# Attention and a gated FFN on one core: fill and first eight slots put in one written step order

## Chip, cores and metric

The kernel runs on one core of a Trainium2 chip. The metric is device time in microseconds for one execution, the median of five runs. The core's engines are named as in the profile: PE is the matrix engine, PEld its weight load, DVE the vector engine, ACT the scalar engine, POOL the GpSimd engine and SP the sync engine. Here POOL mostly issues the input loads, and SP mostly issues transposing transfers and the output.

## What is computed

Two stages follow each other. The first is an attention of two parts on q, k and v of 8 batches, 8 heads, 576 positions and width 64: a full attention on positions averaged by fours, whose output is repeated four times, and a local one in which a position sees those less than four away. Their sum is x, with 4608 rows of 512. The second stage is an FFN with a gate.

```python
def _attn_ref(q, k, v):
    q_d = q.reshape(B, H, Sd, factor, D).mean(axis=3)
    ...
    out_up = np.repeat(sm_attn(q_d, k_d, v_d), factor, axis=2)
    mask = np.abs(pos[:, None] - pos[None, :]) < factor
    scores = np.where(mask, scale * np.matmul(q, k.transpose(0, 1, 3, 2)), -1000000000.0)
    ...
    return (out_up + np.matmul(attn, v)).astype(np.float32)

def _moe_ref(x, w_gate, w_val, w_out):
    gate = np.maximum(x @ w_gate, 0.0)
    val = x @ w_val
    return (gate * val @ w_out).astype(np.float32)
```

`factor` is 4, `d_model` 512 and `d_ff` 1536.

## The kernel before

Two heads make a pair, so there are 32 pairs; four pairs give all 512 columns of x for one batch, 576 tokens. The FFN works on 9 chunks of 512 tokens. A pair goes through these steps:

- **Loads**, on POOL's queue: q and k (for pairs 0 to 8 one transfer each, from pair 9 on one for each head), v in overlapping blocks (`vw`), and from pair 9 on a second copy of v (`v4`) that POOL sums by fours (`emit_v2`, `emit_v1`). Below pair 9 PE does the pooling of v instead, with six matmuls (`emit_vd`, L373) and an ACT copy (L380). The constants `NTP = 9` and `NVP = 9` set the two borders. The weights come in slices, w_gate and w_val in four each (`emit_wslice`, each slice for three of the 12 row blocks jj of the FFN), w_out in four (`emit_wo`).
- **Transposes** of q and k: for pairs 0 to 8 on PE (`emit_qkT_pe`, L328: 24 matmuls into three PSUM banks, with the pooled columns beside the wide ones), evicted by ACT and DVE in six copies (L348 the pooled, L350 the wide ones); from pair 9 on by a transposing transfer from SP (L302), and DVE pools (L309).
- **Scores** (`emit_s1_mm`, L389 and L400), exponentials on ACT (L410 twice for the local part, L424 once for the pooled one, `ed`), the band masks on DVE (L416 twice).
- **Sums**, in one of three forms. For pairs 0 to 3, the fill, `emit_s2`: matmuls with the exponentials as the stationary side (L447 and L456), DVE's reciprocals and products (L464, L465, L472, L474), then `emit_x_pe` transposes x on PE (L601, L605) and copies it to `xT` (L614, L615, L617). For pairs 4 to 8 `emit_s2t`: denominators and numerators side by side (L486 to L514), ln and exp on ACT for the inverse (L523, L525), a product on DVE (L528). From pair 9 on `emit_s2w_mm`, one matmul group for both (L552, L560) with ln, exp and product on L570, L575 and L579. `emit_xsum` (L538) adds the repeated part into `xT`.

A block jj of the FFN is four matmuls with w_gate (hg) and four with w_val (hv), all L622, a relu on ACT (L639) and a gate product on DVE (L643) into `gT`. The output y is 12 matmuls for 128 tokens (L652) in chunk 0; from chunk 1 on it is made by units of seven smaller products with prepared sums (L712, L718), for which DVE prepares differences of w_out halves once (`emit_wt`, L685).

The order of the work is written by functions in the first part. `emit_fill` runs pairs 0 to 3 one after the other, each with loads for four pairs ahead, scores, sums, the next pair's transposes, and matmuls on zeros (`emit_warm`, L825, 512 columns into bank 7) as fillers. `emit_slot` runs slots 0 to 7, one a pair, with three jj blocks of chunk 0 in slots 0 to 3 and of chunk 1 in slots 4 to 7, and the outputs of chunk 0 in slots 4 to 7; slot 7 ends with the list `LEAD_IN`. From slot 8 on the list `ORDER` gives the step order of all engines for two slots at a time (`emit_periods`), and `TAIL` that of the end. Each engine runs its own instructions in the order in which they are written. Queues of loads are POOL's own order.

Outputs of chunk 0 are issued from ACT (`nc.scalar` in `emit_y`); those of units from SP. PSUM has eight banks; the fill uses bank 2 to 5 for scores, 2 to 4 for the transposes of the next pair, 6 for v and the pooled sums, and 0 and 1 for the local sums and for x.

Of the kernel before, what the change touches and what calls it, by code (L numbers as in the profile page):

```python
# [17 lines left out]
LEAD_IN = """  # L18
hg/3 relu/3 o/b00 o/b01 o/b10 o/b11 ln/b0 ln/b1 hv/3 gate/3 inv/b hg/4 relu/4 hv/4 xn/b0 gate/4
hg/5 relu/5 hv/5 xn/b1 xsum/b  # L20
# [35 lines left out]
LATE = ("gate/5/1", "next/0/1", "next/1/1")  # L56
# [61 lines left out]
def kernel(  # L118
# [26 lines left out]
    NVP = 9  # L145
# [10 lines left out]
    ffn = ctx.enter_context(tc.tile_pool(name="ffn", bufs=3))  # L156
# [38 lines left out]
    q32 = q32full[0:96]  # L195
    gT = ring(2, [128, NJJ, TCH], FP16, "gT_")
# [3 lines left out]
    wt4 = [xT[:, 0:3, 0:TCH].rearrange("p k (h d) -> p k h d", h=2)]  # L200
    wt4 += [t.rearrange("p (k h) d -> p k h d", h=2) for t in wtnew]
# [42 lines left out]
    def emit_load_qk(hp):  # L244
        for i in range(4):
            emit_load_q1(hp, i)

    def emit_load_q1(hp, i):

        b, off = head_off(hp)  # L250
        src, dst, hh = (q, k)[i // 2], qk16[hp % NL][:, i // 2, :], i % 2
        if hp < NTP:
            if hh:
                return
            if hp == 0 and src is q:
                nc.sync.dma_start(
                    q32.rearrange("p (n d) -> p n d", d=64),
                    _dap(src, off, [[D, 96], [NQ * D, 2 * NB], [1, D]]),
                )
                nc.scalar.copy(out=dst, in_=q32)  # L260
            else:
                nc.gpsimd.dma_start(
                    dst.rearrange("p (n d) -> p n d", d=64),
                    _dap(src, off, [[D, 96], [NQ * D, 2 * NB], [1, D]]),
                )
            return
        nc.gpsimd.dma_start(  # L267
            dst.rearrange("p (j h d) -> p j h d", h=2, d=64)[:, :, hh, :],
            _dap(src, off + hh * S * D, [[D, 96], [NQ * D, NB], [1, D]]),
        )  # L270
# [45 lines left out]
    def emit_qkT_pe(hp, b0, b1, b0_last=False):  # L316
        r, r4, r2 = hp % NL, hp % 4, hp % 2
        sv = qk16[r].rearrange("p i (h j d) -> p i h j d", h=2, d=64)
        blocks = list(range(2 * NB))
        if hp == 0:  # L320
            blocks = blocks[NB:] + blocks[:NB]
        elif b0_last:
            blocks = blocks[4:] + blocks[:4]
        for n in blocks:
            lo = 120 * (n % 4)
            bank = b0 if n < 4 else b1 + n // 4 - 1
# [8 lines left out]
        big = qkT[r4][:, 0 : 2 * S].rearrange("p (b n t) -> p b n t", b=3, n=4)  # L335
        sml = qkd[r2].rearrange("p i t -> p (i t)").rearrange("p (b n t) -> p b n t", b=3, n=4)
        act, dve = nc.scalar.copy, nc.vector.tensor_copy
        if hp == 0:
            plan = ((2, 1, act), (2, 0, act), (1, 1, dve), (1, 0, dve), (0, 1, act), (0, 0, dve))
        elif b0_last:  # L340
            plan = ((1, 1, act), (1, 0, act), (2, 1, dve), (2, 0, dve), (0, 1, dve), (0, 0, act))
        else:
            plan = ((0, 1, act), (0, 0, act), (1, 1, dve), (2, 1, dve), (2, 0, dve), (1, 0, act))
        for i, pooled, copy in plan:
            bank = b0 if i == 0 else b1 + i - 1
            t = ps[:, bank, 0:480].rearrange("p (n t) -> p n t", n=4)
            if pooled:
                copy(out=sml[:, i], in_=t[:, :, 96:120])  # L348
            else:
                copy(out=big[:, i], in_=t[:, :, 0:96])  # L350
# [16 lines left out]

    def emit_vd(hp, bank):
        t = vw[hp % NL][:, :, 0:64].rearrange("p (h j) d -> p j h d", h=2)
        o = ps[:, bank, 0:256].rearrange("p (c h d) -> p c h d", c=2, h=2)  # L370
        for c in range(2):
            for sig in range(3):
                nc.tensor.matmul(  # L373
                    out=o[:, c, :, :],
                    lhsT=pool_sb[0:WK, sig, :],
                    rhs=t[:, 3 * c + sig, :, :],
                    start=(sig == 0),
                    stop=(sig == 2),
                )
        nc.scalar.copy(  # L380
            out=vd[hp % 3].rearrange("p c (x d) -> p c x d", x=3)[:, :, 0:3:2, :], in_=o[0:72]
# [49 lines left out]
    def emit_s1(hp, p0):  # L431
        emit_s1_mm(hp, p0)
        for g in range(2):
            emit_exp(hp, p0, g)
            emit_mask(hp, g)
        emit_ed(hp, p0)

    def emit_s2(hp, bank, pu):
        r2 = hp % 2
        x = xo[hp % 3]  # L440
        vflat = vw[hp % NL].rearrange("p b c -> p (b c)")
        for hh in range(2):
            for tcx in range(2):
                for c in range(2):
# [4 lines left out]
                        lhsT=ed[r2][:, hh, s0 : s0 + 128],  # L449
# [3 lines left out]
                    )  # L453
        for hh in range(2):
            for j in range(NB):
                nc.tensor.matmul(  # L456
                    out=ps[:, 2 * pu + hh, 65 * j : 65 * j + 65],
                    lhsT=ee[r2][:, hh, NQ * j : NQ * j + 128],
# [4 lines left out]
        rd = small.tile([72, 2, 2], FP32, name="rd", tag="rd")  # L463
        nc.vector.reciprocal(out=rd, in_=_sap(ps, (0, 72), 512 * bank + 64, [[66, 2], [65, 2]]))  # L464
        nc.vector.tensor_tensor(  # L465
            out=x[0:72, NB : NB + 2, :].rearrange("p t (h d) -> p h t d", h=2),
            in0=_sap(ps, (0, 72), 512 * bank, [[131, 2], [65, 2], [1, 64]]),
            in1=_sap(rd, (0, 72), 0, [[2, 2], [1, 2], [0, 64]]),
            op=ALU.mult,
        )  # L470
        ru = small.tile([96, 2, NB], FP32, name="ru", tag="ru")
        nc.vector.reciprocal(out=ru, in_=_sap(ps, (0, 96), 1024 * pu + 64, [[448, 2], [65, NB]]))  # L472
        for j0, j1 in ((0, 3), (3, 6)) if hp == LEAD - 1 else ((0, 6),):
            nc.vector.tensor_tensor(  # L474
                out=x[:, j0:j1, :].rearrange("p j (h d) -> p h j d", h=2),
                in0=_sap(ps, (0, 96), 1024 * pu + 65 * j0, [[513, 2], [65, j1 - j0], [1, 64]]),
                in1=_sap(ru, (0, 96), j0, [[NB, 2], [1, j1 - j0], [0, 64]]),
                op=ALU.mult,
            )

    def emit_s2t_mm(hp, den, num):
        r2 = hp % 2
        e, d = ee[r2], ed[r2]
        for g in range(2):
            for hh in range(2):
                nc.tensor.matmul(  # L486
                    out=ps[64 * hh : 64 * hh + 64, den + g, 0:288],
                    lhsT=ones_sb[0:WK, 0:64],
                    rhs=e[:, hh, 288 * g : 288 * g + 288],
# [3 lines left out]
            for c in range(2):  # L493
                for hh in range(2):
                    nc.tensor.matmul(
                        out=ps[64 * hh : 64 * hh + 64, den + g, 288:360],
                        lhsT=ones_sb[0:72, 64:128],
                        rhs=d[:, hh, c * SD + 72 * g : c * SD + 72 * g + 72],
                        start=(c == 0),
                        stop=(c == 1),  # L500
                    )
        for g in range(2):
            for j in range(3):
                for hh in range(2):
                    nc.tensor.matmul(
                        out=ps[64 * hh : 64 * hh + 64, num + g, NQ * j : NQ * j + NQ],
                        lhsT=vw[hp % NL][:, NB * hh + 3 * g + j, 0:64],
                        rhs=e[:, hh, 288 * g + NQ * j : 288 * g + NQ * j + NQ],
                        start=True,
                        stop=True,  # L510
                    )
            for c in range(2):
                for hh in range(2):
                    nc.tensor.matmul(  # L514
                        out=ps[64 * hh : 64 * hh + 64, num + g, 288:360],
                        lhsT=vd[hp % 3][:, c, 128 * hh : 128 * hh + 64],
                        rhs=d[:, hh, c * SD + 72 * g : c * SD + 72 * g + 72],
                        start=(c == 0),
                        stop=(c == 1),
                    )  # L520

    def emit_rden(den, between=lambda: None):
        nc.scalar.activation(out=rden, in_=ps[:, den : den + 2, 0:360], func=AF.Ln)  # L523
        between()
        nc.scalar.activation(out=rden, in_=rden, func=AF.Exp, scale=-1.0)  # L525
# [3 lines left out]

    def emit_s2t(hp, between):  # L530
        emit_s2t_mm(hp, 4, 2)
        emit_rden(4, between)
        emit_xn(2)
        emit_xsum(hp)
# [51 lines left out]
    def emit_s2w(hp):  # L586
        for hh in range(2):
            for g in range(2):
                emit_s2w_mm(hp, hh, g)
        for hh in range(2):  # L590
            emit_ln(hh)
        emit_inv()
        for hh in range(2):
            emit_xnw(hh)

    def emit_x_pe(hp, pp):
        b, kk = hp // NPB, hp % NPB
        x = xo[hp % 3]
        for g in range(2):
            flat = pair(pp)[:, g, 0:288]  # L600
# [595 lines left out]
```

## Time and profile before

| | |
|---|---|
| median of 5 runs | 348.01 us (346.79 to 348.7) |
| profiled execution | 348.01 us, span 346.0 us |
| PE / DVE / ACT / POOL busy | 336.7 / 293.3 / 215.3 / 192.6 us |
| L622 with w_val / w_gate | 432 and 352 matmuls of 512 columns |
| chain that ended last | PE 84%, DVE 9%, ACT 3%, DMA 2% |
| granted PE clock | 1.000 |
| loads on the software queue (POOL) | 22.93 MB |

A row of a timeline is: start in us, length in us, engine, line, operation, output, inputs, count. A row can merge several instructions of one kind; its length then runs from the first start to the last end, and since an engine begins the next instruction before the last has wholly ended, differences of starts are the better price of an instruction on a full engine. A row of the chain of waits is start, length and the step that held the end at that time. A row of the issue table gives the transfers under way in the stretch asked for, and the time from issue to landing.

### The profile page before, as it was taken

What the parts mean: (1) busy time and instruction counts of PE and PEld (TensorE: products, weight loads), DVE (VectorE), ACT (ScalarE), POOL (GpSimd) and SP (SyncE); (2) the same over time, 40 slices, a digit from 0 to 9 for tenths busy, and PEclk for the clock granted to TensorE, in tenths of its full rate; (3) what the DMA queues carried; (4) which work ended last, traced back from release to release, by engine and by line L of the source; (5) the groups of instructions that cost most, each with busy time, mean ns of one, the idle gap of its engine ahead of it and who ended that gap; (6) DMA issues with size and microseconds to landing.
All of it is one profiled execution on the core that took longest, in us unless ns stands there. A gap on an engine that the chain in (4) does not pass through costs nothing.

```text
span 346.0 us, 8159 instructions
## 1 busy us (share of the span) xinstructions
PE 336.7 (97%) x3187; PEld 210.5 (61%) x3187; DVE 293.3 (85%) x529; ACT 215.3 (62%) x410; POOL 192.6 (56%) x233
## 2 busy tenths in 40 slices
PE   6899999999999999999999999999999999999996
PEld 2665555555565756565666556665766557767685
DVE  5895567788899999999999999999999798786892
ACT  3767776677667776577667766776677634344222
POOL 8986556899989997989298869840300000000000
PEclk9999999999999999999999999999999999999999
DMA  9999999999999999999989998992000001011023
GB/s 151 166 171 186 186 190 160 170 149 189 185 142 188 116 171 120 135 150 145 120 108 164 132 133 77 176 114 66 31 32 31 32 0 47 30 33 52 32 69 109
DMA packets 168774, 40.31 MB, mean 117 GB/s; under 512 B 150080, under 2 KB 165664, under 8 KB 168736
## 3 DMA queue, kind: packets, MB, share of 16 engines
q0 software_dynamic: 132960, 22.93, 92.6%
q1 hardware_dynamic: 35056, 15.79, 23.8%
q10 hardware_dynamic: 720, 1.08, 1.0%
q8 instruction: 25, 0.41, 0.5%
q14 instruction: 13, 0.11, 0.1%
HBM read 46.45 MB, written 9.44 MB: 162 GB/s over the span
## 4 chain that ended last, share of the span: by engine, by line
PE 84%; DVE 9%; ACT 3%; DMA 2%; issue 1%; ACTq 0%; POOLq 0%
PE ps L622 45%; PE ps L718 18%; PE ps L928 4%; PE ps L652 3%; PE ps L552 3%; DVE xo L712 2%; PE ps L328 2%; PE ps L389 2%; PE ps L400 2%; DMA qk<-in_k_dram 2%; PE ps L560 1%; DVE gT L643 1%; ACT rden L570 1%; DVE xn L579 1%; DVE xo L474 1%
## 5 line engine op out<-in xcount | busy, mean ns | idle before, releaser
L622 PE MATMUL ps<-xT,wv_sb 128*128 128x512 f16 x432 | 109.3, 379 | 0.1
L622 PE MATMUL ps<-xT,wg_sb 128*128 128x512 f16 x352 | 89.1, 380 | 0.1
L639 ACT ACTIVATE r<-ps 128x512 f16<-128x512 f32 x88 | 52.3, 595 | 28.2 <-PE ps L622 28.0
L643 DVE TENSOR_TENSOR gT<-r,ps 128x512 f16<-128x512 f16 x88 | 59.2, 681 | 11.6 <-ACT r L639 6.3
L622 PEld LDWEIGHTS <-wv_sb 128*128 128x128 f16 x432 | 41.0, 98 | 41.9 <-issue 0.6
L622 PEld LDWEIGHTS <-wg_sb 128*128 128x128 f16 x352 | 32.0, 98 | 32.3 <-DVE xT L615 0.6
L579 DVE TENSOR_TENSOR xn<-ps,rden 64x720 f16<-64x720 f32 x46 | 41.7, 906 | 6.6 <-ACT rden L575 5.5
L410 ACT ACTIVATE ee<-ps 112x576 f16<-112x576 f32 x64 | 38.1, 648 | 10.4 <-PE ps L400 9.3
L570 ACT ACTIVATE rden<-ps 64x720 f32<-64x720 f32 x46 | 35.2, 765 | 14.9 <-PE ps L560 13.9
L267 POOL DMA_DIRECT2D qk<-in_q_dram x46 | 33.9, 742 | 5.0 <-DMA wo_sb<-in_moe_w_out_dram 2.9
L361 POOL TENSOR_TENSOR vd<-v 72x256 f16<-72x256 f32 x23 | 19.8, 872 | 28.7 <-PE ps L560 28.2
L267 POOL DMA_DIRECT2D qk<-in_k_dram x46 | 33.9, 741 | 2.6 <-DMA v<-in_v_dram 1.1
L416 DVE TENSOR_TENSOR ee<-ee,cst_sb 112x576 f16<-112x576 f16 x64 | 31.3, 511 | 3.0 <-ACT ee L410 2.2
L718 PEld LDWEIGHTS <-gT 128*128 128x128 f16 x288 | 28.2, 98 | 8.6
L292 POOL DMA_DIRECT2D vw<-in_v_dram x30 | 28.7, 956 | 8.4 <-PE ps L622 2.9
L355 POOL TENSOR_TENSOR v<-v 72x512 f32<-72x512 f16 x23 | 31.5, 1370 | 2.0 <-DMA v<-in_v_dram 1.5
L309 DVE TENSOR_REDUCE qkd<-qkT 128x288 f16<-128x1152 f16 x23 | 30.9, 1343 | 0.0
L718 PEld LDWEIGHTS <-xo 128*128 128x128 f16 x240 | 22.6, 98 | 8.1 <-issue 1.7
L752 ACT COPY q<-ps 128x256 f32<-128x256 f32 x39 | 14.5, 372 | 18.8 <-PE ps L718 18.5
L718 PE MATMUL ps<-wo_sb,gT 128*128 128x256 f16 x192 | 24.9, 273 | 0.0
L538 DVE TENSOR_TENSOR xT<-xn 128x576 f16<-128x576 f16 x28 | 24.1, 860 | 0.6
L938 ACT COPY vw<-ps 128x256 f32<-128x256 f32 x30 | 10.8, 374 | 20.7 <-PE ps L928 13.8
(115 smaller groups left out, 572.1 us busy)
## 6 DMA issues: line engine op xcount, KB each, us to landing
out_dram<-y_sb SPq DMA_DIRECT2D x20, 256.0 KB, 3.6
vw<-in_v_dram POOLq DMA_DIRECT2D x30, 168.0 KB, 6.9
qk<-in_q_dram POOLq DMA_DIRECT2D x46, 72.0 KB, 6.2
qk<-in_k_dram POOLq DMA_DIRECT2D x46, 72.0 KB, 6.4
v<-in_v_dram POOLq DMA_DIRECT2D x23, 144.0 KB, 6.6
out_dram<-y_sb SPq DMA_DIRECT2D x22, 128.0 KB, 1.7
wg_sb<-in_moe_w_gate_dram POOLq DMA_DIRECT2D x4, 384.0 KB, 9.6
wv_sb<-in_moe_w_val_dram POOLq DMA_DIRECT2D x4, 384.0 KB, 10.8
```

The costliest lines, as they stand in the source:

```text
L267: nc.gpsimd.dma_start(dst.rearrange("p (j h d) -> p j h d", h=2, d=64)[:, :, hh, :], _dap(src, off + hh * S * D, [[D, 96], [NQ * D, NB], [ ...
L292: nc.gpsimd.dma_start(t, _dap(v, base, [[D, WK], [NQ * D, n], [1, D]]))
L309: nc.vector.tensor_reduce(out=qkd[hp % 2].rearrange("p i t -> p (i t)"), in_=qkT[hp % 4][:, 0 : 2 * S].rearrange("p (t f) -> p t f", f=4), ...
L355: nc.gpsimd.tensor_tensor(out=m, in0=t[:, :, 0:128], in1=t[:, :, 128:256], op=ALU.add)
L410: nc.scalar.activation(out=o, in_=ps[0:WK, p0 + 2 * g : p0 + 2 * g + 2, 0:288], func=AF.Exp, scale=scale)
L416: nc.vector.tensor_tensor(out=o, in0=o, in1=_sap(masks_sb, (0, WK), 288 * g, [[0, 2], [1, 288]]), op=ALU.mult,)
L570: nc.scalar.activation(out=rden[lo : lo + 64], in_=ps[de : de + 64, 4 + 2 * hh : 6 + 2 * hh, 0:360], func=AF.Ln)
L579: nc.vector.tensor_tensor(out=xn[lo : lo + 64], in0=ps[lo : lo + 64, 4 + 2 * hh : 6 + 2 * hh, 0:360], in1=rden[lo : lo + 64], op=ALU.mult,)
L622: nc.tensor.matmul(out=pair(pp)[:, which, :] if out is None else out, lhsT=w[:, kk, bass.ts(jj, 128)], rhs=xT[:, kk, c * TCH : (c + 1) * TCH],
L639: nc.scalar.activation(out=r1, in_=pair(pp)[:, 0, :] if h1 is None else h1, func=AF.Relu)
L643: nc.vector.tensor_tensor(out=gT[c % 2][:, jj, :], in0=r1, in1=pair(pp)[:, 1, :] if h2 is None else h2, op=ALU.mult)
L718: nc.tensor.matmul(out=out, lhsT=left[:, i, :], rhs=right[i], start=(first and i == 0), stop=(i == NK - 1), skip_group_check=True,)
```

## The change

The two lists of functions (`emit_fill`, `emit_slot`, `emit_slot_in`, `LEAD_IN`) are replaced by one list, `FRONT`, in which every step of the fill and of slots 0 to 7 stands by itself: its kind, the pair or jj block, the part, and the PSUM bank. `emit_front` reads it in order. Steps that carry an @ are those of `ORDER`, with the half and the chunk. The list's beginning, which covers the fill and the start of chunk 0, and some later pieces:

```diff
+FRONT = """
+pads loadk/0 loadv/0 loadq/1 loadk/1 loadv/1 loadq/2 cast loadk/2 tr/0/2/4 tr/0/1/3 ev/0/21V/4
+loadv/2 tr/0/0/2 ev/0/20V/4 ev/0/11A/3 vd/0/6 ev/0/01A/2 ev/0/00A/2 loadq/3 vc/0/6 ev/0/10A/3
+warm/6 tr/1/0/7 loadk/3 ev/1/01A/7 ev/1/00A/7 warm/3 tr/1/1/0 loadv/3 s1/0/2 ev/1/11A/0
+ev/1/10A/0 tr/1/2/1 ed/0/2 wg/0 ev/1/20V/1 ex/0/0/2 warm/4 sd/0/6 ev/1/21V/1 wv/0 rd/0/6
+ex/0/1/2 warm/2 s1/1/0 td/0/6 ma/0/0 ones/4 vd/1/6 ex/1/1/0 ma/0/1 loadq/4 warm/2 su/0/4 ed/1/0
+ru/0/4 ex/1/0/0 tu/0/1/4 loadk/4 warm/3 tr/2/1/2 tr/2/2/3 tu/0/0/4 ev/2/10A/2 tr/2/0/0 loadv/4
+ev/2/20V/3 ev/2/11A/2 xp/0/1/5 ev/2/01A/0 xp/0/0/4 ev/2/00A/0 ev/2/21V/3 xe/0/1V/5 vc/1/6 ones/5
+warm/2 s1/2/0 ma/1/1 xe/0/0A/4 ma/1/0 sd/1/6 loadq/5 ex/2/1/0 su/1/4 rd/1/6 td/1/6 ed/2/0 ru/1/4
...
+ex/3/0/0 warm/2 hv/0/0/7 wv/1 hv/0/1/7 tu/2/0/4 ex/3/1/0 hv/1/0/1 hv/1/1/1 ma/3/0 xp/2/0/4
+ones/6 vc/3/6 ma/3/1 xp/2/1/5 xe/2/0A/4 sd/3/6 xe/2/1V/5 tr/4/0/0 loadq/6 rd/3/6 su/3/4
+ev/4/00A/0 td/3/6 tr/4/1/2 ru/3/4 ev/4/01A/0 loadk/6 hg/0/0/6 tu/3/0/4 ev/4/11A/2 hg/0/1/6
+ev/4/10A/2 hv/1/2/1 tu/3/1/4 hg/1/0/0 loadv/6 tr/4/2/3 xp/3/0/4 ev/4/21V/3 xp/3/1/5 xe/3/0A/4
+hg/0/2/6 wg/2 xe/3/1V/5 hg/1/1/0 hg/1/2/0 ev/4/20V/3 hg/0/3/6 wv/2 hg/1/3/0 relu/0/6 hv/0/2/7
+hv/0/3/7 s1/4/2 relu/1/0 gate/0/7 loadq/7 hv/1/3/1 ed/4/2 vd/4/6 hv/2/*/7 ex/4/0/2 ex/4/1/2
+hg/3/*/0 loadk/7 vc/4/6 ma/4/1 tr/5/1/3 ma/4/0 relu/3/0 tr/5/0/2 tr/5/2/4 ev/5/00A/2 hg/2/*/6
+ev/5/21V/4 gate/1/1 ev/5/01A/2 loadv/7 ev/5/10A/3 num/4/0/2 ev/5/20V/4 relu/2/6 vd/5/1 den/4/1/5
+wg/3 vc/5/1 gate/2/7 den/4/0/4 ev/5/11A/3 hv/3/*/1 ln/4 wv/3 num/4/1/3 inv gate/3/1 tr/6/1/0
+s1/5/4 loadq/8 xn/2 tr/6/2/1 ed/5/4 ev/6/21V/1 hg/4/*/2 ex/5/0/4 ev/6/20V/1 ex/5/1/4 loadk/8
...
```

A tr step is a third of a pair's transposes, ev an eviction (block, pooled or not, A for ACT or V for DVE, bank), s1 scores, ex, ed and ma the exponentials and masks, vd and vc the pooling of v and its copy, sd and su the two kinds of sums of the fill, rd, td, ru and tu its reciprocals and products, xp and xe the transposed x and its copy by halves, den and num the two halves of the second form of the sums.

Further on, the loads of w_out stand as wo/0, wo/1, wo/2, then q and k of pair 9, then wo/3, v of pair 8 and v of pair 9. The other edits:

```diff
-LATE = ("gate/5/1", "next/0/1", "next/1/1")
+LATE = ("gate/5/1", "gate/4/1", "next/0/1", "next/1/1")
...
-    NVP = 9
+    NVP = 11
...
-    wt4 = [xT[:, 0:3, 0:TCH].rearrange("p k (h d) -> p k h d", h=2)]
-    wt4 += [t.rearrange("p (k h) d -> p k h d", h=2) for t in wtnew]
+    wt4 = [t.rearrange("p (k h) d -> p k h d", h=2) for t in wtnew]
+    wt4 += [xT[:, 0:3, 0:TCH].rearrange("p k (h d) -> p k h d", h=2)]
...
+    def emit_flip(hp, i, bank):
+        sv = qk16[hp % NL].rearrange("p i (h j d) -> p i h j d", h=2, d=64)
+        for n in range(4 * i, 4 * i + 4):
...
+    def emit_flipped(hp, i, pooled, eng, bank):
...
+        t = ps[:, bank, 0:480].rearrange("p (n t) -> p n t", n=4)
+        copy_on(eng)(out=o[:, i], in_=t[:, :, 96:120] if pooled else t[:, :, 0:96])
...
+    def emit_tu(hp, g, bank):
+        j = 3 * g
+        nc.vector.tensor_tensor(
+            out=xo[hp % 3][:, j : j + 3, :].rearrange("p j (h d) -> p h j d", h=2),
...
+    def emit_x_out(hp, g, eng, bank):
+        lo = hp // NPB * S + 288 * g
+        copy_on(eng)(out=xT[:, hp % NPB, lo : lo + 288], in_=ps[:, bank, 0:288])
...
-        emit_out(c, ty, y_sb, nc.scalar)
+        emit_out(c, ty, y_sb, nc.sync)
...
-    def emit_warm(n):
+    def emit_warm(n, wide=False):
         for _ in range(n):
             nc.tensor.matmul(
-                out=ps[:, 7, :], lhsT=zero_sb[:, 0:128], rhs=zero_sb[:, 128:640], start=True, stop=True
-            )
+                out=ps[:, 7, :] if wide else ps[:, 6, 264:512],
+                lhsT=zero_sb[:, 0:128],
+                rhs=zero_sb[:, 128 : 640 if wide else 376],
...
+    def emit_front(tok):
+        kind, *a = tok.split("/")
+        if "@" in tok:
+            emit_step(kind, a[0], *map(int, a[1].split("@")))
         else:
...
+            FRONT_STEPS[kind](*[int(x) if x.isdigit() else x for x in a])
...
-        emit_warm(10)
-        emit_qkT_pe(0, 2, 3)
-        emit_pads()
-        emit_warm(3)
-        for hp in range(LEAD):
-            emit_fill(hp)
-        gate = None
-        for s in range(PS):
-            gate = emit_slot(s, gate)
+        emit_warm(12, True)
+        for tok in FRONT.split():
+            emit_front(tok)
         emit_periods(PS // 4, (NP - LEAD) // 4)
```

The list also holds the loads that `ORDER` had placed ahead of slot 8, so `emit_periods` starts at its own first chunk. `ORDER` and `TAIL` keep their text; the second gate product of a chunk, gate/4, now comes from `ORDER` at the chunk's border too, as gate/5 did before. The buffers of the relu and of the reciprocals become fixed rings of three and two.

## Prediction before the result was known

> **What bounds the kernel now.** I read the page's head and shares first, then a table of busy time by stretches.
>
> ```profile
> span 346.0 us, 8159 instructions
> PE 336.7 (97%) x3187; PEld 210.5 (61%) x3187; DVE 293.3 (85%) x529; ACT 215.3 (62%) x410; POOL 192.6 (56%) x233
> ...
> 14.40:18.40 4.00, 3.79 (x78) 2.86 (x78) 3.91 (x11) 3.10 (x8) 4.00 (x5) 1.00 1.63 191
> 18.40:22.40 4.00, 3.80 (x78) 2.87 (x78) 3.91 (x11) 3.05 (x8) 3.19 (x5) 1.00 2.13 167
> 46.00:54.60 8.60, 8.60 (x106) 4.56 (x103) 5.76 (x13) 6.82 (x14) 4.52 (x6) 1.00 1.38 200
> 87.00:95.50 8.50, 8.50 (x70) 4.35 (x65) 7.29 (x10) 6.32 (x10) 8.48 (x12) 1.00 1.70 184
> ```
>
> The columns after the length are PE, PEld, DVE, ACT, POOL busy, clock, DMA. From 27 us on PE is bound by its own work (8.60 of 8.60). In the fill, rows one and two, PE looks busy, but part of it are matmuls on zeros; there DVE is full: 3.91 of 4.00. So the front can gain only in the fill, and loses wherever the new order makes PE wait later. DVE's timeline over one pair of the fill:
>
> ```profile
> 16.58 0.17 DVE L464 RECIPROCAL rd<-ps 72x4 f32<-72x4 f32 x1
> 16.78 0.42 DVE L465 TENSOR_TENSOR xo<-ps,rd 72x256 f16<-72x256 f32 x1
> 17.12 0.22 DVE L472 RECIPROCAL ru<-ps 96x12 f32<-96x12 f32 x1
> 17.38 0.95 DVE L474 TENSOR_TENSOR xo<-ps,ru 96x768 f16<-96x768 f32 x1
> 18.25 0.81 DVE L416 TENSOR_TENSOR ee<-ee,cst_sb 112x576 f16<-112x576 f16 x2
> 19.09 0.76 DVE L617 CAST xT<-ps 128x576 f16<-128x576 f32 x1
> 19.76 0.41 DVE L348 CAST qkd<-ps 128x96 f16<-128x96 f32 x2
> 20.09 0.55 DVE L350 CAST qkT<-ps 128x384 f16<-128x384 f32 x1
> 20.55 0.17 DVE L464 RECIPROCAL rd<-ps 72x4 f32<-72x4 f32 x1
> ```
>
> Each starts as the one before ends; the pace is 20.55 - 16.58 = 3.97 us a pair. Start differences are the prices below: pair of masks 0.84, numerators 0.87, xT 0.67, two pooled evictions 0.33, a wide one 0.46. The ends of the two halves of the front, from the chain of waits and PE's timeline:
>
> ```profile
> 26.89 0.47 DVE xT L615
> 27.40 0.61 PE ps L622 x2
> ...
> 95.53 0.82 PE L718 MATMUL ps<-wo_sb,gT 128*128 128x256 f16 x6
> ```
>
> Pair 3's x is complete at 27.36; the first matmul behind slot 7 starts at 95.53. All behind that keeps its text, so the forecast is where this start moves to. The profiled execution took 348.01 us, which is also the median of the runs; 2.0 us of it lie around the span. Loads, from POOL's timeline and the issue table of two short windows:
>
> ```profile
> 4.14 0.88 POOL L262 DMA_DIRECT2D qk<-in_k_dram  x1
> qk<-in_k_dram POOLq DMA_DIRECT2D x1, 144.0 KB, 5.6
> ...
> 19.40 0.83 POOL L794 DMA_DIRECT2D wg_sb<-in_moe_w_gate_dram  x1
> wg_sb<-in_moe_w_gate_dram POOLq DMA_DIRECT2D x1, 384.0 KB, 9.4
> ```
>
> Pair 1's k lands at 4.14 + 5.6 = 9.74, the second w_gate slice at 19.40 + 9.4 = 28.8. POOL's order is unchanged as far as pair 8's k, so these times hold for the changed kernel.
>
> **The first pair of the fill.** In the new order PE takes two of pair 1's transposes ahead of pair 0's scores, and the second reads k. So the scores wait: 9.74 + 0.25 (8 of 24 transposes at 0.75) = 10.0, against 8.89. Then ACT, from its starts: pair 1's two evictions 0.57 after transposes and latency, to 10.8; exp of ed 0.55; two exps 0.55 and 0.65, to 12.55; last mask 13.25; 12 matmuls 0.38 and latency, 13.85; reciprocal 0.25; two half numerators 0.47 each (the two at 24.83 took 0.94). That is 15.05, against 14.35 (13.40 + 0.95): **0.7 lost**, and queued behind it is all of DVE's work for pair 1.
>
> **The pace.** Of a pair's 3.97 DVE gives one pooled eviction to ACT (-0.16) and half of xT (0.67 to 0.39, -0.28); splitting the numerators costs 0.94 for 0.87 (+0.07): 3.60. Pairs 1 and 2 take 7.20, pair 3, with no wide eviction before its numerators, 2.97: 25.2. Its x blocks share banks with the numerators, so both run after: two of 0.25, latency 0.15, xT 0.46: 26.3. **Gained 1.05** on 27.36. ACT, at 3.1 of 4.0, takes what DVE gives (0.14 + 0.40) and is at 3.6, as full as DVE: that cover is thin (first rival).
>
> **Work taken forward.** By 27.40 PE had done 6 matmuls of the first FFN chunk (3 w_val, 3 w_gate); the new order has 11 before pair 3's x: 5 x 0.216 = **1.08 gained**. It is possible because the partial sums get banks 7, 1, 6, 0.
>
> **Work added.** Pairs 9 and 10 pool v on PE: 2 x 0.34 (6 matmuls, from the chain) = 0.68 lost, and two ACT copies of 0.37 beside it. Pair 8 takes the form with 20 matmuls in 0.79 instead of 0.89: -0.10. POOL loses two v4 loads and two pairs of sums (2 x (0.74 + 1.17 + 0.88) = 5.6 us) and the DMA queue 288 KB; PE waited for none of these, so nothing. Each switch from 128-wide work to 64-wide (scores, transposes, pooled sums) costs PE 0.09 (36.26 after 1.83 for 1.74 of matmuls); I count 17 before behind 27.4 and 21 after: +0.36.
>
> **Waits added.** Behind pair 3 the order is followed with the same prices. hg/3 stands before hg/2 and needs the slice that lands at 28.8; PE reaches it at 26.3 + 9 x 0.216 + scores 0.5 + v pooling 0.34 + a switch 0.09 = 29.2, so the load costs nothing, but is also a **floor**: no faster fill would help by more than 0.4. One wait stands out: hg/4 writes bank 2, which xn of pair 4 reads; xn waits for ln and inverse (0.77 + 0.81) behind a relu, an eviction and den/4: about 0.5 lost, and tr/6, vd/6 queue behind. If hg/4 were covered it would cost 0, if ln came one relu later 1.1. The remaining places have 0 to 1 us of slack; v of pair 8, now behind w_out, lands near 57.6 (k of pair 8 at 36.38 + 10.4 = 46.8, then the 7.7 us that w_out takes, 2.0 of pair 9, 1.1 of its own), and by the matmuls ahead of it is read near 58.7.
>
> **Sum.** Start of the first unit: 95.53 - 1.05 - 1.08 + 0.68 - 0.10 + 0.36 + 0.5 = 94.84. That keeps, unexplained, 0.8 us that the old front loses (68.13 from 27.40, against 17 x 0.09 and 65.8 of matmuls: 186 FFN ones at 0.2165, 48 of y at 0.217, 8 scores at 0.505, 4 transposes at 0.75, 5 v poolings at 0.34, 5 sums at 0.80 and 3 at 0.79). If those losses belong to the old order, it is 94.0. I take 94.1: they sit in slots 5 to 7, on rows whose order is rewritten. That is 1.4 earlier: 348.0 - 1.4 = **346.6**, its own range 345.7 to 347.4. Costed at nothing: output copies issued from SP instead of ACT (0.34 x 4, ACT idle at 38%; SP has only the transposes and they are not waited for); bigger zero block at the start (12 for 10, ending near 6.1, before k lands at 6.7); other places of the w_out differences.
>
> **Fillers and clock.** Zero matmuls go from 19 of 512 columns (4.1 us) to 29 of 248 (3.0 us). The granted clock is 1.00 in every row above, at 95% PE busy; after the change PE has some 20 us of work for the 22.4 us to hg/3, about 90%. The Trainium skill speaks against thinning: "TensorE: Matmul & The Clock Gate", part on the clock gate, says that an idle window of about 3.4 us halves the clock. No gap here comes near it, so I put it at 0; by that rule one lost window would cost an estimated 1.7 us, giving 348.3.
>
> **Shared bank 6.** The fillers move from bank 7 to the upper half of bank 6, where ed's sums are read by DVE. "PSUM — Partial Sum Buffer", section on bank collisions, says two engines must not touch one bank in the same partitions at once, so fillers and readers would have to take turns; an estimate of two fillers between rd/0 and td/0 gives 0.2. No row of this trace shows such turn-taking, since bank 7 has no reader; the sum leaves it out.
>
> **Rivals.** (1) *The ring through banks 0 to 3 replaces DVE in the fill, slower.* Scores, exps, transposes and evictions of the next pair all use banks 0 to 3 and mostly ACT: 0.6 + 1.75 + 0.35 + 1.15 + v copy 0.35 + xT 0.40 = 4.6 us a pair if nothing overlaps, 3.6 if all does. At 4.6 for pairs 1 and 2 and 3.6 for pair 3: 15.05 + 9.2 + 3.6 + 1.1 = 28.95, 2.65 later than forecast: 349.3. It decides from about 4.5 on. For it: ACT waits 0.57 for PE in each old pair. Against: old pairs had the same ring and DVE still set the pace. (2) *No change: the slots lose it in waits.* I count nine places with under 0.3 us of slack (vd/5, hv/3, s1/5, tr/6, both den/4 among them); 0.15 each is 1.35, giving 348.0; pair 8's v landing 2 us late would do the same. For it: in-order queues and prices from an older order. (3) *More gain:* hg/4's wait does not come and the 0.8 goes: 28.9 (the floor) + 62.6 + 19 switches 1.7 = 93.2, so 345.7 or a little less (62.6: the 65.8 less 14 FFN matmuls, one scores and one v pooling, with two v poolings more). (4) *It does nothing:* all in the PE-bound part is the same work; then only pooling, pair 8 and switches show (+0.68 - 0.10 + 0.36), 348.9.
>
> **How the numbers follow.** Forecast 0.45; rival 1 0.14; rivals 2 and 4 together 0.28; rival 3 0.13. 0.3% of 348.0 is 1.04 us: faster means below 346.97, slower above 349.05. Of the forecast's case four fifths are faster (0.37), all of rival 3, a little of rival 2: 0.53. Slower: most of rival 1, 0.13. Same: 0.34. The range 345.2 to 348.9 leaves out about 0.05 below and 0.14 above.
>
> **What would show it.** Right: tu of pair 0 ends near 15.0; 3.6 a pair on DVE; last xT near 26.3; hg/3 near 29.2; a PE gap before hg/4; the first unit near 94.1, and nothing changed behind it. Wrong: ACT, not DVE, full at 15 to 25; PE gaps over 0.2 behind 30; a half clock; vd/8 waiting for its load; or a first unit that is early while the rest of the span grows.

## The result and the profile after

The changed kernel takes **349.98 us** (median of 43 runs, 348.6 to 355.18) against 347.83 us of the kernel before (80 runs): ratio 1.0065, 95% interval 1.0052 to 1.0077. The forecast was 346.6, so even the sign was wrong, and the time lies above the upper bound of the range. Three executions of the changed kernel at 355 us ran at a lower mean clock (0.979 and 0.986) and are not in the ratio. The profiled execution took 350.33 us with a span of 348.5.

The page's head, its share line, and four stretches of the changed kernel (length, then PE, PEld, DVE, ACT, POOL busy, clock, DMA share, GB/s), the last one moved by 4.3 us so that it ends where the first unit starts:

```profile
span 348.5 us, 8161 instructions
PE 338.5 (97%) x3199; PEld 211.8 (61%) x3199; DVE 291.7 (84%) x530; ACT 217.7 (62%) x419; POOL 185.3 (53%) x227
...
14.40:18.40 4.00, 3.60 (x83) 2.88 (x84) 3.07 (x9) 3.26 (x9) 4.00 (x5) 1.00 1.74 188
18.40:22.40 4.00, 3.48 (x79) 2.77 (x76) 3.67 (x12) 3.12 (x10) 3.10 (x5) 1.00 2.05 170
46.00:54.60 8.60, 8.60 (x107) 4.50 (x105) 6.37 (x13) 5.85 (x11) 5.26 (x7) 1.00 1.51 194
91.30:99.80 8.50, 7.62 (x52) 3.76 (x51) 7.25 (x10) 5.55 (x9) 8.47 (x10) 1.00 1.93 192
```

DVE is relieved in the fill (3.07 and 3.67 of 4.00, before 3.91), as meant, but the fill did not become faster (table below). And the last row shows something new: PE, which was never idle in the stretch before the first unit, stands still for 0.9 of 8.5 us. The start of the first unit, from PE's timeline, is 4.3 us later than before (95.53):

```profile
99.85 0.82 PE L721 MATMUL ps<-wo_sb,gT 128*128 128x256 f16 x6
```

What PE waited for, from the view of waits by engine (total, times, longest):

```profile
PE ps L583 <- DVE ee L452: 1.9, 3, 0.9
...
PE ps L809 <- ACT vd L415: 0.5, 1, 0.5
PE ps L809 <- DVE xo L502: 0.4, 1, 0.4
PE ps L809 <- DVE rd L497: 0.3, 1, 0.3
PE ps L637 <- DVE xn L565: 0.3, 1, 0.3
```

Two kinds are new. The **fillers** (L809) wait for ACT and DVE; in the kernel before no filler of the fill had a wait worth listing. And sums (L583) wait for masks (L452): two of the three waits lie ahead of the first unit (pairs 9 and 11, 0.72 and 0.88), the third, 0.34, behind it.

To compare executions I split each trace by four marks: the start of the first transposes (when pair 0's k has landed), the end of pair 3's last xT, the start of the first unit, the end. The first mark differs between executions of the same program (6.28 to 7.47 us in all that I profiled), so the length from it is what counts.

| us | first transposes | to last xT | to first unit | to the end |
|---|---|---|---|---|
| before | 6.79 | 20.55 | 68.19 | 250.49 |
| before, again | 7.16 | 20.87 | 69.03 | 249.39 |
| after | 7.03 | 21.64 | 71.18 | 248.64 |
| after, again | 6.28 | 21.95 | 71.66 | 248.69 |

The change loses 1.1 us in the fill and 3.0 in the slots, though five FFN matmuls (1.08 us) have moved out of the slots into the fill; it is 1.85 shorter behind. Between the second executions the differences are 1.08, 2.63 and 0.70.

### The profile page after: what moved, and what is told of

Same layout as the page of the kernel before. It is cut to its first block, busy times and chain, and to the rows that moved or that the text cites. A ratio compares the mean times of both kernels' runs of the same rounds, so it can differ in the third digit from the quotient of the medians.

```text
span 348.5 us, 8161 instructions
## 1 busy us (share of the span) xinstructions
PE 338.5 (97%) x3199; PEld 211.8 (61%) x3199; DVE 291.7 (84%) x530; ACT 217.7 (62%) x419; POOL 185.3 (53%) x227
## 4 chain that ended last, share of the span: by engine, by line
PE 87%; DVE 5%; ACT 4%; DMA 2%; issue 1%; ACTq 0%; DVEq 0%; POOLq 0%
PE ps L637 46%; PE ps L721 20%; PE ps L902 4%; PE ps L583 4%; PE ps L653 2%; PE ps L436 2%; PE ps L425 2%; DVE ee L452 2%; PE ps L591 2%; PE ps L362 2%; DMA qk<-in_k_dram 2%; PE ps L406 1%; PE ps L809 1%; ACT rden L601 1%; DVE xT L569 1%
## 5 line engine op out<-in xcount | busy, mean ns | idle before, releaser
L637 PEld LDWEIGHTS <-wv_sb 128*128 128x128 f16 x432 | 40.3, 98 | 39.9 <-issue 0.3
L601 ACT ACTIVATE rden<-ps 64x720 f32<-64x720 f32 x48 | 36.7, 765 | 18.3 <-PE ps L591 17.4
L610 DVE TENSOR_TENSOR xn<-ps,rden 64x720 f16<-64x720 f32 x48 | 43.5, 905 | 5.0 <-ACT rden L606 3.8
L452 DVE TENSOR_TENSOR ee<-ee,cst_sb 112x576 f16<-112x576 f16 x64 | 33.4, 540 | 7.5 <-ACT ee L446 6.8
L390 POOL TENSOR_TENSOR vd<-v 72x256 f16<-72x256 f32 x21 | 18.3, 880 | 26.6 <-PE ps L591 26.2
L384 POOL TENSOR_TENSOR v<-v 72x512 f32<-72x512 f16 x21 | 26.9, 1279 | 3.2 <-DMA v<-in_v_dram 2.7
```

Source lines behind the costliest of these rows:

```text
L452: nc.vector.tensor_tensor(out=o, in0=o, in1=_sap(masks_sb, (0, WK), 288 * g, [[0, 2], [1, 288]]), op=ALU.mult,)
L601: nc.scalar.activation(out=rden[lo : lo + 64], in_=ps[de : de + 64, 4 + 2 * hh : 6 + 2 * hh, 0:360], func=AF.Ln)
L610: nc.vector.tensor_tensor(out=xn[lo : lo + 64], in0=ps[lo : lo + 64, 4 + 2 * hh : 6 + 2 * hh, 0:360], in1=rden[lo : lo + 64], op=ALU.mult,)
L637: nc.tensor.matmul(out=out, lhsT=w[:, kk, bass.ts(jj, 128)], rhs=xT[:, kk, c * TCH : (c + 1) * TCH], start=(kk == 0), stop=(kk == 3),)
```

## The experiments

### The fillers: left out, or moved to another bank

The theory: fillers in bank 6, where ed's sums and v's pooling are read, take turns with the readers. First all 29 fillers of the changed kernel's fill were left out:

```diff
-warm/6 tr/1/0/7
+tr/1/0/7
...
-warm/3 tr/1/1/0
+tr/1/1/0
...
-warm/4 sd/0/6
+sd/0/6
...
```

> The changed kernel without the 29 matmuls on zeros of the fill (the twelve wide ones at the start stay). Theory: in the fill these fillers share bank 6 with the v sums, and fillers and readers of that bank wait for each other (0.53, 0.34 and 0.42 us of PE and 0.46 of DVE in its trace); without them pair 3's x is ready about 1.6 us earlier, and the time falls from 1.0065 of before to about 1.002. Rival: the fillers only fill waits that come from DVE; then nothing changes, 1.0065 within 0.0012. Second rival: without them the granted clock falls in the fill and the time grows.

Measured: 351.38 us, ratio to the kernel before 1.01 (1.0052 to 1.0149). The stretches of the fill:

```profile
6.00:10.00 4.00, 2.53 (x48) 1.60 (x46) 0.72 (x2) 2.00 (x7) 4.00 (x5) 0.97 2.43 155
10.00:14.00 4.00, 3.80 (x59) 2.98 (x58) 2.06 (x6) 3.10 (x8) 4.00 (x6) 0.50 2.43 155
14.00:18.00 4.00, 3.97 (x62) 3.37 (x59) 3.02 (x8) 3.06 (x9) 4.00 (x6) 0.50 1.88 182
```

The clock (third number from the right) is 0.50 from 10 us on, and comes back only at 27; the mean clock of its six executions is 0.974 to 0.990. So this run does not show what the fillers' place costs: without them the fill takes 24.49 us instead of 21.64. It does show that the fillers are needed.

So the second run keeps them, in bank 7, where nothing is read in the fill. The three between pair 1's first and second transposes go, since bank 7 then holds those transposes:

```diff
-                out=ps[:, 7, :] if wide else ps[:, 6, 264:512],
+                out=ps[:, 7, :] if wide else ps[:, 7, 264:512],
...
-warm/6 tr/1/0/7 loadk/3 ev/1/01A/7 ev/1/00A/7 warm/3 tr/1/1/0 loadv/3 s1/0/2 ev/1/11A/0
+warm/6 tr/1/0/7 loadk/3 ev/1/01A/7 ev/1/00A/7 tr/1/1/0 loadv/3 s1/0/2 ev/1/11A/0
```

> The changed kernel with 26 of the 29 fillers in bank 7, which nothing reads after pair 1's first transposes; the three between pair 1's transposes are left out. Theory (sharing of bank 6): as without fillers, about 1.002 of before. If the fillers cost by their own 0.1 us each instead, this stays near 1.0065 while the kernel without fillers is faster.

Measured: 348.57 us, ratio 1.0016 (0.9988 to 1.0045), clock 1.00. Fill 20.23 us after the first transposes; the slots, with the slow masks that the next section is about, still take 70.79. The same steps of pair 0 in the timelines of the two kernels, first the changed one:

```profile
8.40 0.38 ACT L415 CAST vd<-ps 72x256 f16<-72x256 f32 x1
8.82 0.80 PE L809 MATMUL ps<-zero_sb 128*128 128x248 f16 x6 [0.53 <-ACT vd L415]
...
12.49 0.18 DVE L497 RECIPROCAL rd<-ps 72x4 f32<-72x4 f32 x1 [0.20 <-ACT ee L446]
12.73 0.37 PE L809 MATMUL ps<-zero_sb 128*128 128x248 f16 x2 [0.34 <-DVE rd L497]
...
13.14 0.42 DVE L502 TENSOR_TENSOR xo<-ps,rd 72x256 f16<-72x256 f32 x1 [0.46 <-PE ps L809]
```

and with the fillers in bank 7:

```profile
7.66 0.80 PE L809 MATMUL ps<-zero_sb 128*128 128x248 f16 x6
7.86 0.37 ACT L415 CAST vd<-ps 72x256 f16<-72x256 f32 x1
...
11.09 0.38 PE L809 MATMUL ps<-zero_sb 128*128 128x248 f16 x2
11.36 0.18 DVE L497 RECIPROCAL rd<-ps 72x4 f32<-72x4 f32 x1 [0.20 <-ACT ee L446]
11.58 0.42 DVE L502 TENSOR_TENSOR xo<-ps,rd 72x256 f16<-72x256 f32 x1
```

Above, the last column of brackets shows a chain in both directions: filler waits for the copy of v, two more wait for the reciprocal, and the product td then waits for the fillers. Below, copy and fillers overlap (7.66 to 8.46 and 7.86 to 8.23), and td follows the reciprocal at once. The Trainium skill ("PSUM — Partial Sum Buffer", section "PSUM bank collisions raise a hardware error") says that two engines must be kept apart on one bank in the same partitions even at different addresses; the turn-taking in these rows is what that looks like in a program that does keep them apart.

Then the same bank in the kernel before: fillers of 248 columns, twice as many, once in bank 6 and once, as a control, in bank 7.

```diff
+    def emit_warm6(n):
+        for _ in range(2 * n):
+            nc.tensor.matmul(
+                out=ps[:, 6, 264:512], lhsT=zero_sb[:, 0:128], rhs=zero_sb[:, 128:376],
...
-        emit_warm(3 if hp == 0 else 2)
+        emit_warm6(3 if hp == 0 else 2)
```

> The kernel before, its fill fillers put where the changed kernel has them: the upper half of bank 6, 248 columns wide and twice as many, so that PE multiplies about as many zeros. Theory: fillers and the readers of bank 6 take turns, in any order of steps: waits of fillers for vd's copy (ACT) and for td (DVE), last xT 1.4 to 2.4 us later than 27.3, ratio 1.005. Rival: the loss in the changed kernel's fill was its new order, and the bank costs nothing: last xT within 0.3 of 27.3, ratio 1.000.

> Control for the fillers in bank 6: the kernel before with the same fill fillers, 248 columns wide and twice as many, left in bank 7, which nothing reads. Theory: what stopped the clock in the other run were the fillers' waits for readers of their bank, so here clock 1.00 in every slice, last xT within 0.3 of 20.55 us after the first transposes, ratio 1.000. Rival: narrow fillers hold the clock badly by themselves: clock near 0.5 in the fill, ratio over 1.02.

Measured: bank 6 361.31 us, ratio 1.0386 (1.0356 to 1.0416); bank 7 347.6 us, ratio 1.001 (0.9982 to 1.0038), fill 20.55 us, exactly as before. In bank 6 far more happens than either theory expected. PE's timeline, then two stretches:

```profile
9.02 0.51 PE L373 MATMUL ps<-vw,cst_sb 112*128 112x128 f16 x6
...
10.96 1.15 PE L831 MATMUL ps<-zero_sb 128*128 128x248 f16 x6 [1.43 <-ACT vd L380]
```

```profile
10.00:14.00 4.00, 3.04 (x42) 2.40 (x42) 1.33 (x5) 2.00 (x6) 4.00 (x6) 0.66 2.44 155
14.00:18.00 4.00, 2.90 (x38) 2.09 (x36) 2.77 (x7) 1.98 (x4) 4.00 (x6) 0.50 1.75 186
```

In the old order ACT copies v only behind the exponentials, so the filler, and PE behind it, waits 1.43 us for the copy; the clock falls to 0.50 at 11.2 us and stays there until 38.5, while the next pairs wait in the same place. The fill takes 34.88 us. The mechanism is confirmed, in another order of steps; its size there is mostly that of the clock: PE's waits over 0.1 us in the fill add up to 5.41 us against 1.64 in the kernel before, 3.8 of the 14.3 lost.

### POOL's sums moved off the masks

The other theory: in slots 5 to 7 of the changed kernel, masks and the repeated part (xsum) run beside POOL's sums of v and are slowed. All engines' timeline of the changed kernel, only the rows that matter:

```profile
91.53 1.67 DVE L569 TENSOR_TENSOR xT<-xn 128x576 f16<-128x576 f16 x1
92.54 2.03 POOL L384 TENSOR_TENSOR v<-v 72x512 f32<-72x512 f16 x1
93.12 1.76 DVE L452 TENSOR_TENSOR ee<-ee,cst_sb 112x576 f16<-112x576 f16 x2
...
94.94 0.29 PE L583 MATMUL ps<-ee,vw 112*128 112x96 f16 x3 [0.88 <-DVE ee L452]
```

Two masks take 1.76 here and 0.81 in the fill; xsum 1.67, elsewhere 0.75; PE waits for the second mask. Three sums were put later in POOL's order, nothing else:

```diff
-o/b01/0@1 v2/b/0@1 o/b10/0@1
+o/b01/0@1 o/b10/0@1
...
-y/3/1/1 v1/a/1@1 relu/3/0@1
+y/3/1/1 relu/3/0@1
...
-qk/a1/1@1 y/2/1/0
+qk/a1/1@1 v2/b/0@1 v1/a/1@1 y/2/1/0
...
-v2/a/1@1 o/b00/1@1
+o/b00/1@1
...
-v/b/1@1 inv/b/1@1
+v/b/1@1 v2/a/1@1 inv/b/1@1
```

> The changed kernel with POOL's v sums for pairs 11 and 12 put a few loads later in POOL's order, away from the masks of pairs 9 and 11. Theory: a mask of 0.45 us took 1.2 to 1.4 beside a POOL sum, and PE waited 0.72 and 0.88 us for the masks; without that the masks take 0.45, both waits go, and the time falls by about 1.6 us to 1.002 of before. Rival: the waits are the order's own, the masks come late whatever POOL does: less than 0.4 us.

Measured: 347.94 us, ratio 1.0016 (0.999 to 1.0042). From last xT to first unit 69.16 us instead of 71.18; the fill keeps its 21.64. The same place:

```profile
88.22 1.17 POOL L385 TENSOR_TENSOR v<-v 72x512 f32<-72x512 f16 x1
89.47 0.71 POOL L391 TENSOR_TENSOR vd<-v 72x256 f16<-72x256 f32 x1
91.08 0.74 DVE L570 TENSOR_TENSOR xT<-xn 128x576 f16<-128x576 f16 x1
91.89 0.83 DVE L453 TENSOR_TENSOR ee<-ee,cst_sb 112x576 f16<-112x576 f16 x2
```

The sums now run beside products that read PSUM (88.22 falls into two products of 0.90 each, their usual length), and xsum and masks are back at 0.74 and 0.83. The Trainium skill states the rule: "SBUF — State Buffer", section "Who interferes with whom", says that a DVE instruction with two SBUF inputs contends with a GpSimd instruction that reads SBUF, and that one with at most one, outside the two-port modes, does not. The rows agree for masks and products. Two rows go further: in the two executions of the kernel before a mask (at 88.8 and at 90.7) took 1.41 and 1.40 beside POOL's load issues alone, as far as POOL's rough spans show, and in the second PE waited 0.50 for it.

### Both repairs together

> The changed kernel with both repairs: fillers in bank 7 (three dropped) and the three pooled sums on POOL moved off the masks. Theory: the two losses are separate, one in the fill and one in slots 5 to 7, so both go: last xT 26.6 as with the fillers moved, 69.2 us from there to the first unit as with the sums moved, first unit near 95.8, 248.1 behind it, span 343.9, ratio to the kernel before 0.996. Rival: POOL's sums keep their own time (its loads set it) while PE now comes 2 us earlier, so they meet other masks: first unit near 97.4, ratio 1.001.

Measured: **346.79 us, ratio 0.9977 (0.9959 to 0.9995)**. This is below both kernels, below the kernel before by little. Its marks: first transposes 7.31, fill 20.33, slots 69.15, behind 249.21. In this execution each repair's part is there in full (21.64 to 20.33, 71.18 to 69.15), so the two losses are separate. The last changed kernel under "Behind the first unit" has the same front and does not keep all of the second. The expected 343.9 for the span came out as 346.0: the first k landed 0.9 later than in the run with bank 7, and 249.2 instead of 248.1 behind.

### What cutting the transposes costs

The new order cuts transposes and sums into pieces between FFN blocks. In the kernel before the transposes in slots 1 to 3 were cut in three, with the next block's hg and hv between:

```diff
-            emit_qkT_pe(hp + 1, 4, 0, True)
-        return emit_h(c, jj + 2, 3)
+            emit_qkT_pe(hp + 1, 4, 0, True, (lambda: emit_h_mm(c, jj + 2, 3, 0, range(4)),
+                                             lambda: emit_h_mm(c, jj + 2, 3, 1, range(4))))
+            return emit_h(c, jj + 2, 3, ())
```

> The old kernel with the transposes of slots 1 to 3 cut in three, four FFN matmuls between the pieces, as the new order has them; nothing else changes. Theory: each excursion of PE from 128-wide to 64-wide work and back costs 0.21 us, so six more cost 1.2 us: 1.0035 of before. Rival: the switch is free where nothing waits: 1.000 within 0.001.

Measured: 351.85 us, ratio 1.0114 (1.0069 to 1.0158), three times what was expected. PE's timeline before and with the cuts, over the same work:

```profile
38.59 0.82 PE L328 MATMUL ps<-cst_sb,qk 96*64 96x120 f16 x24
39.34 1.04 PE L622 MATMUL ps<-xT,wg_sb 128*128 128x512 f16 x4
40.22 1.03 PE L622 MATMUL ps<-xT,wv_sb 128*128 128x512 f16 x4
41.08 0.50 PE L373 MATMUL ps<-vw,cst_sb 112*128 112x128 f16 x6
```

```profile
39.05 0.40 PE L330 MATMUL ps<-cst_sb,qk 96*64 96x120 f16 x8
39.38 1.04 PE L624 MATMUL ps<-xT,wg_sb 128*128 128x512 f16 x4
40.35 0.40 PE L330 MATMUL ps<-cst_sb,qk 96*64 96x120 f16 x8
40.68 1.04 PE L624 MATMUL ps<-xT,wv_sb 128*128 128x512 f16 x4
41.65 0.40 PE L330 MATMUL ps<-cst_sb,qk 96*64 96x120 f16 x8
41.98 0.51 PE L375 MATMUL ps<-vw,cst_sb 112*128 112x128 f16 x6
...
42.91 0.31 PE L488 MATMUL ps<-ee,ones_sb 112*64 112x288 f16 x2 [0.42 <-ACT qkT L352]
```

The same matmuls take 41.08 - 38.59 = 2.49 us in one piece and 41.98 - 39.05 = 2.93 in three: 0.44 for two more excursions into 64-wide work, **0.22 each**. My term was 0.09, read from the way in alone (here 39.38 to 40.35, 0.97 for four FFN matmuls of 0.2165); the other 0.12 or so is the way back, which lies in the 0.33 from transposes to the next FFN matmul. The rest of the 3.49 us that the slots lost (71.68 for 68.19) is mostly the edit's own fault: denominators now wait for evictions that come late (0.42, 0.42 and 0.86 in the three slots), and the sums of one slot wait 0.26 for a mask beside POOL's sums. The fill lost 0.83 in this execution too, which the edit does not touch: its first 24 transposes took 1.41 us instead of 0.82. So the run gives the price of a switch, not an estimate of the change.

### Behind the first unit

I had written that nothing would change there; after is 1.85 us shorter than before. In before's timeline PE waited 0.67 and 0.65 us for a y addition queued behind differences (L712) that took 1.50 beside POOL's sums instead of 0.55. The first of the two places:

```profile
136.76 1.46 POOL L355 TENSOR_TENSOR v<-v 72x512 f32<-72x512 f16 x1
137.14 1.50 DVE L712 TENSOR_TENSOR xo<-gT,xo 128x768 f16<-128x768 f16 x1
...
140.29 0.81 PE L718 MATMUL ps<-wo_sb,xo 128*128 128x256 f16 x6 [0.67 <-DVE y_sb L767]
```

Two theories: it is a matter of when they meet, or POOL is relieved because pairs 9 and 10 left it. First the pooling alone, in the kernel before:

```diff
-    NVP = 9
+    NVP = 11
...
+            emit_vd(hp, 3)
             emit_h(c, jj, 0)()
             emit_wt(s - 3)
```

> The kernel before with v of pairs 9 and 10 pooled on PE (into bank 3, just ahead of the first FFN step of slots 5 and 6), their v4 loads and sums on POOL gone. Both theories: first unit 0.4 to 0.9 later than 95.5 (two times 0.34 on PE, less what the sums had slowed). They differ behind it. A, what the changed kernel got back behind the first unit is a matter of when POOL's sums meet DVE's differences there: 250.5 stays within 0.6, ratio 1.002. B, it is got back because POOL and the queue have less to do: 248.5, ratio 0.997.

Measured: 349.31 us, ratio 1.006 (1.003 to 1.0091). From last xT to the first unit 68.86 for 68.19: 0.67 for two poolings, as forecast (0.68). Behind it 250.06, and the median is longer, not shorter: nothing here speaks for the relief of POOL. In this execution the differences met the sums at another place:

```profile
102.20 2.40 DVE L712 TENSOR_TENSOR xo<-gT,xo 128x768 f16<-128x768 f16 x1
103.02 1.17 POOL L355 TENSOR_TENSOR v<-v 72x512 f32<-72x512 f16 x1
...
106.25 0.81 PE L718 MATMUL ps<-wo_sb,xo 128*128 128x256 f16 x6 [1.06 <-DVE y_sb L767]
```

Then two of POOL's sums in the repeated order were put later, in the kernel before:

```diff
-v1/a/1 inv/a/0 c22//0 p/4/0 gate/0/0 v2/a/0 p/3/0
+inv/a/0 c22//0 p/4/0 gate/0/0 p/3/0
...
-qk/a2/1 next/0/0
+qk/a2/1 v1/a/1 v2/a/0 next/0/0
```

> The kernel before with one edit in the repeated order: POOL's two sums v1/a/1 and v2/a/0 stand behind qk/a2/1, some 2.2 us later, so that they meet DVE's reduction and the y additions and not the differences of w_out (xo). Theory: the differences that took 1.08 and 1.50 beside these sums take 0.55, the PE waits of 0.7 and 0.6 near 140 and 212 go, behind the first unit 249.2 for 250.5, span 344.7, ratio 0.9965. Rival: the waits were for something else, or come back elsewhere: 250.5, ratio 1.000.

Measured: 349.27 us, ratio 1.0025 (0.9996 to 1.0054): a miss, with 249.68 behind the first unit. The two waits went, but a pair of masks met one of POOL's sums:

```profile
152.09 2.74 DVE L416 TENSOR_TENSOR ee<-ee,cst_sb 112x576 f16<-112x576 f16 x2 [0.25 <-ACT ee L410]
153.16 1.35 POOL L355 TENSOR_TENSOR v<-v 72x512 f32<-72x512 f16 x1
...
154.98 0.29 PE L552 MATMUL ps<-ee,vw 112*128 112x96 f16 x3 [1.13 <-DVE ee L416]
```

The same edit on top of both repairs:

> The changed kernel with both repairs, and POOL's two sums v1/a/1 and v2/a/0 of the repeated order behind qk/a2/1. Theory: behind the first unit PE already runs nearly without waits with the two repairs alone (its waits there are under 0.5 in all), so nothing is to be had: ratio to the kernel before 0.998. Rival: the sums still cost DVE time that PE pays for: ratio 0.994.

Measured: 346.85 us, ratio 0.9999 (0.9976 to 1.0022), behind the first unit 247.78 with no wait over 0.1. Not told apart from the version without it, and this time not from the kernel before either.

Ahead of the first unit this kernel has the same text as the one with both repairs, and its fill takes 20.38. But its slots take 70.21, not 69.15. POOL's sum met two masks of another pair:

```profile
80.19 2.81 DVE L453 TENSOR_TENSOR ee<-ee,cst_sb 112x576 f16<-112x576 f16 x2 [0.33 <-ACT ee L447]
80.62 1.16 POOL L385 TENSOR_TENSOR v<-v 72x512 f32<-72x512 f16 x1
...
83.06 0.29 PE L584 MATMUL ps<-ee,vw 112*128 112x96 f16 x3 [0.53 <-DVE ee L453]
```

PE waited 0.20 and 0.53 for them, and the first unit starts at 97.1, near the 97.4 that the rival of the run with both repairs had named. POOL's list is the same up to there, but ahead of this sum POOL waited 2.68 and 1.43 us for loads of v to land, where it waited 0.81 and 0.59 in the run with both repairs, and the sum started at 80.62 instead of 77.57. So the repair of the fill held in all three of its executions; the new place of POOL's sums held in two and not in the third. Whether both repairs together are faster than the kernel before (0.9977 once, 0.9999 once) is not settled.

Last, both kernels unchanged once more:

> The kernel before, unchanged, profiled again. Theory: behind the first unit its 250.5 us hold two PE waits (0.7 and 0.6) that come from where POOL's sums happen to meet DVE's differences, so another execution can show 249 to 250.5 there, and the first k lands between 6.4 and 7.5. Rival: the behind part is fixed by the program: 250.5 within 0.2.

> The changed kernel, unchanged, profiled again. Theory: from the first transposes to the last xT 21.6 us, from there to the first unit 71 (masks beside POOL's sums again), behind it 248 to 249. Rival: the slow masks were chance: 69 to the first unit.

Their marks stand in the table above. The slots of the changed kernel again take 71.7 us, with 2.0 us of waits for masks, so its slow masks are no chance. Over the executions with the new front the slots follow these waits: 71.18 and 71.66 us with 1.60 and 2.00 of them, 70.79 with 1.16 (fillers in bank 7 alone), 70.21 with 0.73, and 69.16 and 69.15 with none. Behind the first unit the kernel before shows 249.39 now, and the control with narrow fillers, whose work there is the same, 248.49. The PE gaps over 0.1 us behind the first unit add up to 1.57 in the first trace of before, 0.91 in the second and 0.30 in the control; 0.34 and 0.43 in the two of after. So most of those 1.85 us are meetings of POOL's sums with DVE that the profiled execution of before happened to have. In all, the part behind takes 248.49 to 250.49 us in six executions with the old front and 248.06 to 249.21 in six with the new one, its text unchanged in each of the two groups. That the changed order meets fewer of them on the median is likely (its time rose by 2.15 us, its first unit by 3 to 5), but why is left open.

## Why the prediction was wrong

Measured from the first transposes, the forecast first unit was 94.1 - 6.79 = 87.3 us; the trace has 99.85 - 7.03 = 92.8. The 5.5 between them:

- **Shared bank 6, "the sum leaves it out": +1.4.** This is the step that failed first. The page's rule was quoted against the change and then left out because no row of the old trace showed it; that trace could not show it, as its bank 7 had no reader. 21.64 against 20.23 and 20.33 with the fillers in bank 7. The prediction's own estimate for it was 0.2. It hit the fill's first pair most: the last tu of pair 0 ended 9.12 after the first transposes, with the bank free 8.18 and 8.28, forecast 8.26.
- **The pace, 3.60, 3.60 and 2.97: +0.8 with what follows the last pair.** Ends of tu in the run with both repairs lie 3.72, 3.82 and 3.16 apart, and the last xT ends 1.35 behind the last of them, forecast 1.1. The working was right, the sizes a little small. So the new fill order alone gains 0.2 to 0.3 us on the old 20.55, not 1.05, though with 11 instead of 6 FFN matmuls done, as forecast.
- **"The remaining places have 0 to 1 us of slack": +2.0.** The slots were worked out with prices from rows without POOL beside them. With POOL's order moved against DVE's, masks of 0.45 became 0.9 to 2.0 in the two executions. I priced only what leaves POOL ("so nothing"), not what the sums that stay would meet. Rival 2 named waits in the slots, but by many small slacks, not by this mechanism. The sign "PE gaps over 0.2 behind 30" did come (0.72 and 0.88).
- **Switches at 0.09, and "if those losses belong to the old order": +1.3.** The switch costs 0.22 in the one run that prices it. Four more of them are 0.9, not 0.36. And the forecast let 0.7 of the old front's unexplained 0.8 vanish (94.1 for 94.84), which did not happen; what that 0.8 consists of stays open. It cannot be 17 switches at 0.22, which is 3.7, since 68.13 exceeds 65.8 by only 2.3: prices such as the 0.75 for the transposes already hold a way back. The split into these two is worked out, not run by itself, and two executions of the kernel before differ by 0.84 in their slots (68.19 and 69.03).

**Right:** first pair of the fill 0.7 later, once the bank is free; pooling of pairs 9 and 10 on PE (0.67 for 0.68); a wait before hg/4 (0.31 for 0.5); no wait for a w_gate slice; clock 1.00 in both profiles of the changed kernel. **Rival 1**, which had the slower side, was not it: ACT was at 3.26 and 3.12 of 4.00 in the fill, not full, and with the bank free a pair took 3.72 to 3.82, not the 4.5 from which it decides. **Rival 4** came near in time (348.9) with another mechanism. "Nothing changed behind it" held for the order, not for the 250.5 us, which was one execution's value. That last error made the forecast's miss smaller: 5.75 us late at the first unit, 1.85 given back, 3.9 in the span.

## What to carry over

When fillers or any idle work get a new PSUM bank, list that bank's readers: a bank with a reader turns the filler into a wait in both directions, and a wait can cost the clock too. When one in-order engine's list is rewritten, price its instructions beside what the other engines will be doing then; here DVE's masks, xsum and differences, with two inputs in SBUF, took some two to four times as long beside POOL's sums, and where they meet differs between executions of one program, so look at more than one. And take the price of a switch between kinds of matmuls from the whole excursion, in and out.

## What was not expected of the hardware

- The clock halved without any long gap. Without fillers PE's longest gap between 6.9 and 10 us was 0.72 us (busy 0.42 and 0.68 of the two microseconds from 8 on) and the clock was 0.50 from 9.8 to 26.9; the kernel before was busy 2.68 of 4.00 us from 6 to 10 and kept 1.00. With fillers waiting in bank 6 of the old kernel gaps of 0.53 and 1.43 were enough. The Trainium skill ("TensorE: Matmul & The Clock Gate", part on the clock gate) speaks of an idle window of about 3.4 us; reading that as one unbroken gap, as the prediction did, is refuted here.
- The kernel before does not always keep its clock. In its second profile PE waited 2.04 us for the first k, and the clock was 0.50 from 7.8 to 11.2 us; the 0.32 by which that fill is longer (20.87 for 20.55) was lost there. That execution's mean clock is 0.994; 28 of the 72 executions of that kernel beside the experiments show 0.994 or 0.995, and none of the 36 of the three kernels with 26 fillers in bank 7 does.
- At half clock PE looks full: 3.97 of 4.00 busy at clock 0.50. Its share alone would have read as a better fill.
- The first k lands 6.28 to 7.47 us after the start in executions of programs with the same first load: 1.2 us that differ between executions before the first transposes start.
